# Turning gathered rows by VectorE after a trip through DRAM, in place of TensorE

## The chip, the cores and the metric

The kernel runs on one core of one Trainium2 chip. The metric is the device time of one launch in microseconds (us): the median of three runs is 1747.23 us (1746.43 to 1751.63). A further execution was recorded by the hardware profiler; all readings of the profile and of the trace are from that one execution.

The core has five instruction streams that run side by side and wait for each other by semaphores: TensorE (PE, with its weight loads shown as PEld), VectorE (DVE), ScalarE (ACT), GpSimd (POOL) and SyncE (SP). In this kernel POOL also issues the indirect DMAs (rows gathered or scattered by index), and SP issues nearly all plain DMAs. Each stream executes its instructions in the order in which they stand in the program.

## The reference

Two parts follow one another: an attention without softmax, and a mixture of eight experts on its result.

```python
scores = scale * np.matmul(z, z.transpose(0, 2, 1))          # 8 batches, 2496 tokens, 64 features
attn = np.maximum(scores, 0.0) ** 2
x = (u * np.matmul(attn, v)).reshape(N, 256)                  # N = 19968 rows

do_compute = (x @ w_skip) > 0                                 # about half of the rows
logits = xc @ w_gate                                          # xc = x[do_compute]
e_idx = np.argmax(logits, axis=1)
gate_w = softmax(logits)[e_idx]
for e in range(8):                                            # rows of one expert
    h = np.maximum(xc[mask] @ w1[e], 0.0)                     # 256 -> 1024
    y[mask] = gate_w[mask, None] * (h @ w2[e])                # 1024 -> 256
out[do_compute] = xc + y                                      # the other rows: out = x
```

## The kernel before

**Number format.** All matmuls work on fp32 values that are split into a high and a low part (tiles ending in `h` and `l`); three products (high by high, low by high, high by low) are accumulated. So whoever makes a matmul operand makes two tiles: a cast on ACT for the high part and a subtraction on DVE (or POOL) for the low part.

**Attention** (the first 1260 us or so). For each batch and each chunk of 512 queries, `scores` (L277), `weights` (L325 to L339) and `attend` (L366) run over the keys; `finish` (L379) multiplies by `u` and stores the rows to `out` and to a DRAM tensor `xr`, from which the second part reads. `kept` holds score blocks in DRAM so that the mirrored half is not computed again. `routing` (L419) finds each row's expert and writes its token number and gate weight into a DRAM list `lst`, one stretch for each expert.

**Experts** (from about 1257 us to the end). For expert `e` (0 to 7 in the code) the rows are handled in *pairs* of 2 x 128 rows. `fetch` (L576) copies the row numbers into `go` on DVE (L580) and gathers the two times 128 rows from `xr` by two indirect DMAs on POOL (L582). They arrive with one row in each partition. The first matmul needs the features in the partitions, so `turn_pe` (L592) turns each pair: four 128 x 128 transposes on TensorE into a PSUM tile `pst` (L600), a cast on ACT into the high part `xh` (L602), a subtraction on DVE into the low part `xl` (L603). The turned pair lies in `xt` or, for pair 0 of an expert, `xtf`.

**A unit** (`unit`, L605) handles up to 512 rows: parts `h_part` (L620: matmuls with `w1` into a PSUM tile `psh`, ReLU on ACT into `hh` L639, low part on DVE into `hl` L640) and `y_part` (L645: matmuls with `w2` L653), lagging by `lead` parts. There are four PSUM buffers for `psh`, so the fifth `h_part` of a unit needs the first `hl`. At the end, DVE makes `o` = gate x y + row (L682) and POOL scatters it to `out` (L685).

**Each expert** has three fixed units of 256 rows (`NFIX` = 3; pairs 0, 1, 2), called units 0, 1 and 2 here. The rest of its rows, whose number is known only at run time, is done in a branch (`tc.Switch`, L970) with one arm for each number of 64-row strips; the arm has one or two units of up to 512 rows, with pairs 3, 4 and, where needed, 5. In this data the arms of experts 1 to 7 have 8, 8, 7, 4+5, 5, 4+5 and 8+4 strips. Every engine takes the branch by itself, on entry and on leaving.

**What sets the order.** The order is written out by hand (`manual_schedule`, L786): each stream executes what the program emits, in the order of emission. `fills` names work that is slipped in between the parts of a unit: `(k, f)` emits `f` after part `k`. A fixed unit has seven parts: h0, h1, h2, h3, y, y, y are k = 0 to 6, and k = 7 stands behind them all but ahead of `o`. Before the change, unit `i` of an expert `e` from 1 on emits:

```python
add(fills, (1, rows(e, i + 3)), (3, lambda: turn_pe(pair(e, i + 1), turned(e, i + 1))))
if more:
    add(fills, (4, rows(e + 1, i)))
...
add(fills, *zip((1, 3, 5), wq[3 * i : 3 * i + 3]))
if e and more and i == 2:
    add(fills, (7, lambda: turn_pe(pair(e + 1, 0), turned(e + 1, 0))))
if i == NFIX - 1:
    add(fills, (5, lambda: turn_pe(pair(e, NFIX + 1), turned(e, NFIX), 2, 2 * P)))
```

`rows` is a `fetch`: pair `i + 3` of this expert and pair `i` of the next are gathered in unit `i`. `wq` are the eight pieces of the next expert's weights (`load_w`, L126): SP loads a piece into one of four `raw` buffers (L97), ACT casts it (L152, L158), and from expert 2's weights on POOL subtracts (L153, L159), which frees the `raw` buffer. So POOL's stream in a fixed unit holds, in this order, a gather of two, weight pieces, a second gather of two, a weight piece, and the two scatters of the unit; SP's stream holds the weight loads, each waiting for a free `raw` buffer, and one load of a list of row numbers.

## Time and profile before

| what | value |
|---|---|
| time, median of 3 runs | 1747.23 us |
| time of the profiled execution | 1763.1 us |
| its span, first to last instruction | 1761.3 us |
| granted TensorE clock | 0.996 |
| TensorE busy | 98% of the span |
| VectorE, ScalarE, GpSimd busy | 68%, 64%, 29% of the span |
| transposes of `turn_pe` on TensorE | 180 (176 into `pst`, 4 into `psm`) |
| DMA, mean over the span | 167 GB/s |

How to read it: "busy" is a share of the whole span and mixes the two parts. In the forty slices of the profile VectorE and ScalarE are at 7 to 8 tenths in the attention and at 3 to 4 in the experts, GpSimd at 1 to 3 and then 3 to 6, TensorE at 9 (that is 90% or more) in nearly all. The profiled execution took 15.9 us more than the median of the timed runs.

### The profile page before, as it was taken

The page shows a single profiled execution, that of the slowest core. Times are in us where ns is not written, and L with a number is a line of the kernel's source. Part 1 is how long each engine was busy: PE and PEld are TensorE (multiplying, and loading weights), DVE is VectorE, ACT ScalarE, POOL GpSimd, SP SyncE. Part 2 cuts the span into 40 slices and gives each one's busy share as a digit, 9 for nine tenths or more (in the row PEclk, how much of TensorE's full clock was granted, in tenths as well). Part 3 has the DMA queues.
Part 4 walks back from the last instruction along what each step waited for, and adds up shares of the span by engine and source line. Part 5 has one row for each costly group of instructions (what it writes and reads, how often), then busy time and mean ns, then how long its engine had stood idle before and what let it go on. Part 6 is the DMA issues. An engine that isn't in the chain of part 4 may idle for free.

```text
span 1761.3 us, 39302 instructions
## 1 busy us (share of the span) xinstructions
PE 1734.3 (98%) x15476; PEld 1548.9 (88%) x15476; DVE 1189.1 (68%) x1928; ACT 1130.9 (64%) x1409; POOL 517.6 (29%) x516
## 2 busy tenths in 40 slices
PE   9999999999999999999999999999899999999998
PEld 7888788988898898888899888888789999999997
DVE  6877877887787788788778877877643333433432
ACT  8877877887788788778777876877333323333321
POOL 1103212211320221232122123112345456645631
PEclk9999999999999999999999999999999999999999
DMA  5676789587778868787785888678452333323210
GB/s 193 150 181 169 193 228 255 136 232 218 206 184 215 244 157 229 224 214 177 210 258 147 225 235 215 154 209 221 133 126 76 79 96 108 87 60 98 85 40 28
DMA packets 454666, 294.71 MB, mean 167 GB/s; under 512 B 218224, under 2 KB 393201, under 8 KB 454352
## 3 DMA queue, kind: packets, MB, share of 16 engines
q1 hardware_dynamic: 440288, 267.86, 57.0%
q0 software_dynamic: 13632, 22.99, 4.7%
q8 instruction: 136, 2.23, 0.5%
q14 instruction: 178, 1.46, 0.3%
q10 hardware_dynamic: 432, 0.18, 0.0%
HBM read 157.47 MB, written 133.79 MB: 165 GB/s over the span
## 4 chain that ended last, share of the span: by engine, by line
PE 86%; DMA 5%; issue 3%; DVE 2%; ACT 2%; SPq 0%; POOL 0%; POOLq 0%; DVEq 0%; ACTq 0%
PE acc L366 53%; PE y L653 11%; PE psh L634 11%; PE ps L277 9%; DMA out<-o,idt 2%; DMA r<-kept 2%; PE psm L434 1%; DVE al L339 1%; ACT ah L335 1%; PE pst L600 1%; DMA raw<-in_v 1%; DMA kept<-rt 1%; ACT r L325 0%; ACT r L326 0%; DVE rt L294 0%
## 5 line engine op out<-in xcount | busy, mean ns | idle before, releaser
L366 PE MATMUL acc<-ah,vh 64*128 64x512 f32 (+1 forms) x3120 | 645.8, 384 | 2.6 <-DVE ah L335 2.0
L366 PE MATMUL acc<-ah,vl 64*128 64x512 f32 (+1 forms) x3120 | 630.6, 382 | 0.0
L339 DVE TENSOR_TENSOR al<-r,ah 128x1024 fp32r<-128x1024 f32 (+1 forms) x400 | 479.3, 1205 | 172.1 <-ACT ah L335 146.2
L366 PE MATMUL acc<-al,vh 64*128 64x512 f32 (+1 forms) x3120 | 500.5, 383 | 1.4 <-DVE al L339 0.5
L533 POOL DMA_INDIRECT lst<-pair,dest x160 | 198.9, 1243 | 776.8 <-DVE dest L531 745.8
L335 ACT CAST ah<-r 128x1024 fp32r<-128x1024 f32 (+1 forms) x356 | 362.6, 1029 | 82.2 <-PE acc L366 39.4
L366 PEld LDWEIGHTS acc<-ah,vh 64*128 64x128 f32 x3120 | 331.4, 184 | 51.6 <-ACT ah L335 4.5
L366 PEld LDWEIGHTS acc<-ah,vl 64*128 64x128 f32 x3120 | 331.6, 184 | 40.3 <-DVE vl L122 0.3
L366 PEld LDWEIGHTS acc<-al,vh 64*128 64x128 f32 x3120 | 314.0, 184 | 51.5 <-DVE al L339 10.1
L325 ACT ACTIVATE r<-ps 128x1024 f32<-128x1024 f32 (+1 forms) x248 | 252.5, 1018 | 143.2 <-PE ps L277 117.7
L639 ACT ACTIVATE hh<-psh 128x512 fp32r<-128x512 f32 (+2 forms) x172 | 96.3, 571 | 296.1 <-PE psh L634 247.5
L326 ACT ACTIVATE r<-r 128x1024 f32<-128x1024 f32 (+1 forms) x248 | 261.4, 1054 | 7.9
L653 PE MATMUL y<-w2t,hh 128*128 128x256 f32 (+1 forms) x1328 | 236.3, 281 | 0.0
L640 DVE SCALAR_TENSOR_TENSOR hl<-psh,hh 128x512 fp32r<-128x512 f32 (+2 forms) x172 | 110.0, 655 | 153.0 <-ACT hh L639 110.5
L294 DVE STREAM_TRANSPOSE rt<-r 128x512 f32<-128x512 f32 x304 | 197.3, 687 | 10.5 <-DMA kept<-rt 10.5
L653 PEld LDWEIGHTS y<-w2t,hh 128*128 128x128 f32 (+1 forms) x1328 | 201.9, 186 | 1.3
L634 PE MATMUL psh<-xt,w1h 128*128 128x256 f32 (+3 forms) x896 | 187.4, 306 | 10.9 <-issue 5.6
L653 PE MATMUL y<-w2t,hl 128*128 128x256 f32 (+1 forms) x664 | 184.8, 278 | 0.0
L634 PEld LDWEIGHTS psh<-xt,w1h 128*128 128x128 f32 x896 | 143.1, 190 | 18.6 <-issue 8.0
L634 PE MATMUL psh<-xt,w1l 128*128 128x256 f32 (+3 forms) x448 | 136.1, 304 | 1.4 <-issue 1.4
L685 POOL DMA_INDIRECT out<-o,idt x77 | 76.3, 991 | 171.4 <-DVE o L682 139.0
L653 PEld LDWEIGHTS y<-w2t,hl 128*128 128x128 f32 (+1 forms) x664 | 123.3, 186 | 0.0
(188 smaller groups left out, 1712.2 us busy)
## 6 DMA issues: line engine op xcount, KB each, us to landing
kept<-rt SPq DMA_DIRECT2D x304, 256.0 KB
r<-kept SPq DMA_DIRECT2D x90, 512.0 KB
r<-kept SPq DMA_DIRECT2D x62, 352.0 KB
raw<-in_v SPq DMA_DIRECT2D x80, 256.0 KB
ut<-in_uT SPq DMA_DIRECT2D x32, 512.0 KB
xr<-xrow SPq DMA_DIRECT2D x128, 128.0 KB
out<-xrow SPq DMA_DIRECT2D x128, 128.0 KB
raw<-in_w SPq DMA_DIRECT2D x64, 256.0 KB
```

The costliest lines, as they stand in the source:

```text
L277: nc.tensor.matmul(to, k[h, o : o + P], queries(ci, q, h, n), start=(m == 0), stop=(m == 2))
L294: nc.vector.transpose(t[:, :, 32 * k : 32 * k + 32].rearrange("p (k a) i -> p a k i", k=4), r[:, x, :].rearrange("p (a k i) -> p a k i", a ...
L325: nc.scalar.activation(r[:, :, :n], ps[:, :, :n], AF.Relu, scale=isc)
L326: nc.scalar.activation(r[:, :, :n], r[:, :, :n], AF.Square)
L335: (nc.scalar.copy if on_act(ci, p) else nc.vector.tensor_copy)(h_, r_)
L339: nc.vector.tensor_sub(l_, r_, f32(h_))
L366: nc.tensor.matmul(acc[t][:, :n], w[h, x, dd], a[h, x, :n], start=(first and t not in halves[:m]), stop=(last and t not in halves[m + 1 :]),)
L533: put = nc.gpsimd.indirect_dma_start(out=lst, out_offset=bass.IndirectOffsetOnAxis(ap=dest[:, t : t + 1], axis=0), in_=pair[:, t, :], in_o ...
L634: nc.tensor.matmul(ps[:, j * W : (j + 1) * W], wt[:, a, o : o + P], x[:, d, :W], start=(m == 0), stop=(m == 5),)
L639: nc.scalar.activation(hh[:, : G * W], ps[:, : G * W], AF.Relu)
L640: nc.vector.scalar_tensor_tensor(hl[:, : G * W], ps[:, : G * W], 0.0, f32(hh[:, : G * W]), op0=ALU.max, op1=ALU.subtract)
L653: nc.tensor.matmul(ys[t], h[:, tt], w2t[f][:, k, :], start=(f == 0 and m == 0 and t % share == 0), stop=(f == NF - 1 and m == 2), skip_gro ...
```

## The change

Pairs of experts 1 to 7 (the second to the eighth) are no longer turned by TensorE. Instead:

- `to_far`: SP stores the gathered pair, as it lies, into a DRAM tile `far[e % 2][i]` of 256 x 256 (one DMA of 256 KB).
- `blocks`: SP loads it back in another order, by four DMAs of 64 KB, one for each group of 64 features, into 32 partitions each (`blk`, three buffers, in the space that `ut` had): partition 32 b + i holds the features 64 b to 64 b + 63 of the rows i, i + 32, i + 64 and so on. Each DMA has 256 pieces of 256 bytes.
- `turn_dve`: DVE transposes 32 x 32 blocks of it into `raw` (128 x 512); then ACT casts and DVE subtracts, as before but from SBUF in place of PSUM.
- the rows of `w1` are permuted on the host for experts 1 to 7, so that the features' order after these blocks fits.

The gathers themselves, their places and POOL's stream stay. Expert 0 keeps `turn_pe`; so does the loop for rows beyond the longest arm, which this data does not reach.

Places: `to_far(e, i + 3)` stands at k = 5 of unit `i` (k = 4 in unit 2), `to_far(e + 1, i)` at k = 6 (k = 7 in unit 2). `blocks(e, i + 1)` stands at k = 0 of unit `i`; in unit 2 also `blocks(e, 4)` at k = 2, `blocks(e + 1, 0)` at k = 4 and `blocks(e, 5)` at k = 6. The turns stay where `turn_pe` stood. All of `to_far` and `blocks` is in SP's stream.

```diff
+    blk = []
+
+    def blocks(e, i):
+        src = far[e % 2][i].rearrange("(m i) (b f) -> b i m f", i=32, b=4)
+        x = blk[1 + (i - 1) % 2 if i else 0].rearrange("p (m f) -> p m f", f=64)
+        for b in range(4):
+            nc.sync.dma_start(x[32 * b : 32 * b + 32], src[b])
+
+    def to_far(e, i):
+        return lambda: nc.sync.dma_start(far[e % 2][i].rearrange("(t p) d -> p t d", p=P), pair(e, i))
+
+    def turn_dve(e, i, xt, o=0):
+        x = blk[1 + (i - 1) % 2 if i else 0].rearrange("p (m d j) -> p m d j", d=2, j=32)
+        raw = zp.tile([P, 2 * D], F32, name="xraw", tag="zf", bufs=3)
+        nc.vector.transpose(raw.rearrange("p (d m i) -> p m d i", d=2, i=32), x)
+        xh, xl = (x[:, :, o : o + UT] for x in xt)
+        r = raw.rearrange("p (d q) -> p d q", d=2)
+        nc.scalar.copy(xh, r)
+        nc.vector.tensor_sub(xl, r, f32(xh))
...
+    def turn(e, i, xt, o=0):
+        return (lambda: turn_dve(e, i, xt, o)) if e else (lambda: turn_pe(pair(e, i), xt, 2, o))
...
             if e:
-                add(fills, (1, rows(e, i + 3)), (3, lambda: turn_pe(pair(e, i + 1), turned(e, i + 1))))
+                add(fills, (0, to_blocks(e, i + 1)), (1, rows(e, i + 3)))
+                add(fills, (3, turn(e, i + 1, turned(e, i + 1))), (4 if i == 2 else 5, to_far(e, i + 3)))
                 if e == 1 and i == 0:
-                    add(fills, (0, rows(1, 2)))
+                    add(fills, (0, rows(1, 2)), (4, to_far(1, 2)))
                 if more:
-                    add(fills, (4, rows(e + 1, i)))
+                    add(fills, (4, rows(e + 1, i)), (7 if i == 2 else 6, to_far(e + 1, i)))
...
-            if e and more and i == 2:
-                add(fills, (7, lambda: turn_pe(pair(e + 1, 0), turned(e + 1, 0))))
+            if e and i == NFIX - 1:
+                add(fills, (2, to_blocks(e, NFIX + 1)), (6, to_blocks(e, NFIX + 2)))
+            if more and i == NFIX - 1:
+                add(fills, (4 if e else 7, to_blocks(e + 1, 0)))
+                if e:
+                    add(fills, (7, turn(e + 1, 0, turned(e + 1, 0))))
             if i == NFIX - 1:
-                add(fills, (5, lambda: turn_pe(pair(e, NFIX + 1), turned(e, NFIX), 2, 2 * P)))
+                add(fills, (5, turn(e, NFIX + 1, turned(e, NFIX), 2 * P)))
...
+    w1 = np.concatenate([moe_w1[:1], moe_w1[1:, cols]])
```

In the last fixed unit of expert 0, `to_far(1, 0)` and `to_far(1, 1)` stand at k = 5 and 7 and `blocks(1, 0)` at k = 7; pair 0 of expert 1 is turned in the first unit of expert 0's arm, at k = 1. In the two-unit arms the pairs of the second unit are turned by `turn_dve` at k = 3 and 5 of the first.

More of the change, by code (lines that the diff above doesn't have):

```diff
@@ L85, in attn_moe @@
     lst = dram.tile([E * CAP, 2], I32, name="lst")
+    far = [[dram.tile([UT, D], F32, name="far%d%d" % (k, i)) for i in range(NSTAT)] for k in range(2)]
     zt, vt = {}, {}
@@ L866, in attn_moe @@
     row_tiles("u", 4)
+    blk += [xp.tile([P, 2, QC], F32, name="blk", tag="ut", bufs=3)[:, 0, :] for _ in range(3)]
     xtf += [zp.tile([P, 2, 2 * P], F32R, name="xtf", tag="zl", bufs=ZBUFS) for _ in range(2)]
@@ L979, in attn_moe @@
             if e == 0 and not ws:
-                turn_pe(pair(1, 0), turned(1, 0))
+                turn(1, 0, turned(1, 0))()
             for j, hw in enumerate(ws):
@@ L985, in attn_moe @@
                 if e == 0 and j == 0:
-                    add(fills, (1, lambda: turn_pe(pair(1, 0), turned(1, 0))))
+                    add(fills, (1, turn(1, 0, turned(1, 0))))
                 while there < min(i + 3, end - 1):
                     there += 1
-                    add(fills, (1, rows(e, there)))
+                    add(fills, (1, rows(e, there)), *([(3, to_far(e, there))] if e else []))
                 if after:
                     xt = xts[(NFIX + j + 1) % 2]
-                    add(fills, (3, lambda nxt=nxt, xt=xt: turn_pe(pair(e, nxt), xt)))
-                    if after[0] > 4:
-                        add(fills, (5, lambda nxt=nxt, xt=xt: turn_pe(pair(e, nxt + 1), xt, 2, 2 * P)))
+                    for k in range(2 if after[0] > 4 else 1):
+                        if e and nxt + k > NFIX + 2:
+                            add(fills, (4 * k, to_blocks(e, nxt + k)))
+                        add(fills, (3 + 2 * k, turn(e, nxt + k, xt, 2 * P * k)))
                 w = -(-hw // 2)
```

23 lines of the change are left out of this document (16 added, 7 removed).

## The prediction

> **What bounds the kernel now.** I read the page's busy line first, then its slices, then the timeline of TensorE in one expert.
>
> ```profile
> PE 1734.3 (98%) x15476; PEld 1548.9 (88%) x15476; DVE 1189.1 (68%) x1928; ACT 1130.9 (64%) x1409; POOL 517.6 (29%) x516
> ...
> PE   9999999999999999999999999999899999999998
> ...
> POOL 1103212211320221232122123112345456645631
> ```
>
> TensorE is busy nearly without a gap, so what is taken from it is won, unless it has to wait for something new. POOL's 29% is an average over two parts; in the experts it is the next fullest. How full it is in the fixed units shows only in the expert itself. I take the fourth expert (e = 3), whose unit 0 begins at 1448.46. Columns of the first row: stretch, length, then busy us of each engine:
>
> ```profile
> 1456.00:1490.00 34.00, 33.23 (x271) 32.54 (x270) 13.07 (x26) 12.34 (x27) 28.93 (x30) 1.00 0.48 132
> ...
> 1448.46 0.40 PE L634 MATMUL psh<-xtf,w1h 128*128 128x256 f32 x2
> ...
> 1456.48 1.05 POOL L582 DMA_INDIRECT xgu<-xr,go  x1 [3.19 <-DVE go L580]
> ...
> 1479.86 1.04 POOL L582 DMA_INDIRECT xgu<-xr,go  x1 [0.31 <-issue]
> 1481.20 1.02 POOL L582 DMA_INDIRECT xgu<-xr,go  x1 [0.30 <-issue]
> ```
>
> POOL has 28.93 us of work in 34, and 0.3 us of issue before each gather or scatter (the last rows), so from 1456.48 on it has nothing to spare. It starts its first gather 8.0 us after TensorE has begun unit 0 (1448.46) and stays that late: the gather of pair 5, emitted after part 1 of unit 2, starts its second half only at 1481.20. Today nobody minds, because pair 5 is turned in the arm or not at all.
>
> Next, the end of unit 2 and the start of the arm on TensorE and VectorE:
>
> ```profile
> 1483.68 0.60 PE L600 MATMUL pst<-ident,xgf 128*128 128x128 f32 x4
> 1484.03 0.65 PE L634 MATMUL psh<-xt,w1h 128*128 128x448 f32 x2
> ...
> 1488.77 0.36 PE L634 MATMUL psh<-xt,w1l 128*128 128x448 f32 x1
> 1489.90 0.67 PE L634 MATMUL psh<-xt,w1h 128*128 128x448 f32 x2 [0.77 <-DVE hl L640]
> ```
>
> ```profile
> 1484.94 0.69 DVE L603 TENSOR_TENSOR xtf<-pst,xtf 128x512 fp32r<-128x512 f32 x1 [1.42 <-ACT xtf L602]
> 1485.54 0.87 DVE L682 SCALAR_TENSOR_TENSOR o<-y,idt,xgf 128x256 f32<-128x256 f32 x2
> 1489.22 2.22 DVE L640 SCALAR_TENSOR_TENSOR hl<-psh,hh 128x448 fp32r<-128x448 f32 x4 [2.81 <-ACT hh L639]
> ```
>
> TensorE goes from unit 2 into the arm without a pause, does the four `h_part`s for which there is PSUM, and then waits for the first `hl`. That comes 4.28 us after VectorE began the low part of `xtf` (1484.94 to 1489.22): the two `o`, and the branch, in which VectorE stands still for 2.81 us though ScalarE was the one named. So the turn of the next expert's pair 0, last before the branch, already decides when TensorE goes on, and TensorE has under a microsecond of slack there (0.77 us lost).
>
> **The change part by part.** *Removed:* the transposes. What a turn costs TensorE is read between neighbours:
>
> ```profile
> 1454.22 0.60 PE L600 MATMUL pst<-ident,xgf 128*128 128x128 f32 x4
> 1454.57 0.48 PE L653 MATMUL y<-w2t,hh 128*128 128x256 f32 x2
> ...
> L600 PE MATMUL pst<-ident,xgf x92: 270/272/328, 1259.3 to 1703.0; 128*128 128x128 f32 x92
> ...
> L600 PE MATMUL pst<-ident,xgu x84: 270/272/273, 1298.0 to 1726.6; 128*128 128x128 f32 x84
> ```
>
> Four transposes take 1454.57 - 1454.22 = 0.35 us of TensorE's stream. 92 + 84 = 176 are 44 turns; four of them (pairs 1 to 4 of expert 0) stay, so 40 go: 40 x 0.355 = 14.2 us, if nothing is put in their place.
>
> *Added on VectorE and ScalarE:* a block transpose a turn, for which the attention has the same shape; the cast and the subtraction stay.
>
> ```profile
> L294 DVE STREAM_TRANSPOSE rt<-r x304: 660/686/714, 46.4 to 1219.1; 128x512 f32<-128x512 f32 x152
> ...
> L602 ACT CAST xt<-pst x37: 582/583/587, 1263.1 to 1727.0; 128x512 fp32r<-128x512 f32 x37
> ```
>
> 0.69 us, five to seven times an expert, on an engine that was busy 13.07 of 34 us: nothing, beside the wait. The cover is the y parts of the same unit.
>
> *Added on SP:* five DMAs a turn, in a stream that so far held only weight loads. These rows price them:
>
> ```profile
> 1389.62 0.97 POOL L685 DMA_INDIRECT out<-o,idt  x1 [0.95 <-issue]
> 1392.29 0.97 POOL L685 DMA_INDIRECT out<-o,idt  x1 [1.70 <-DMA out<-o,idt]
> ...
> 1423.72 3.49 DMA xgu<-xr,go
> ...
> 1248.02 2.21 SPq L412 DMA_DIRECT2D xr<-xrow  x4
> ...
> 1192.73 5.95 DMA r<-kept
> ```
>
> A 128 KB indirect transfer is through 1392.29 - 1389.62 = 2.67 us after its start, or 1.70 us after its issue has ended; a gather that meets the next weights' loads takes 3.49 us (chain of waits). For gathers I take 2.67, as those weight loads now stand behind it in SP's stream. SP issues four stores of 256-byte pieces, of 128 KB each, in 2.21 us, 0.55 each; a load of 64 KB has half the pieces, so four cost between 1.1 and 2.2 us; I take 1.6. The trace has no load of 256-byte pieces. Its landing after the last issue is at least the 1.70 above and at most 5.95 - 0.55 = 5.4 (512 KB in the full queues of the attention); the experts' queues are half empty (DMA share 0.48), so I take 2.2, near the low end.
>
> *The wait.* SP works in order. In unit 2 it has, one behind the other, `blocks(e, 3)`, `blocks(e, 4)`, `to_far(e, 5)`, `blocks(e + 1, 0)`. The third must wait for the gather of pair 5, though the fourth needs nothing of it: its rows were put away two units earlier. And VectorE meets the fourth in the last turn ahead of `o` and the branch. So, with F the start of the second half of that gather:
>
> F + 0.5 (POOL a little later, below) + 2.67 (gather lands) + 0.55 (`to_far` issued) + 1.6 + 2.2 (`blocks(e + 1, 0)`) = F + 7.5: data there. Then 0.69 (block transpose) + 0.59 (cast) + 4.28 (low part, `o`, branch) = F + 13.1: first `hl` of the arm. For e = 3: 1481.20 + 13.1 = 1494.3 instead of 1489.22, 5.1 us late. The other experts, by their own rows:
>
> ```profile
> 1366.32 1.01 POOL L582 DMA_INDIRECT xgu<-xr,go  x1 [0.30 <-issue]
> ...
> 1425.07 1.01 POOL L582 DMA_INDIRECT xgu<-xr,go  x1 [0.30 <-issue]
> ...
> 1539.50 1.01 POOL L582 DMA_INDIRECT xgu<-xr,go  x1 [0.30 <-issue]
> ...
> 1602.33 1.01 POOL L582 DMA_INDIRECT xgu<-xr,go  x1 [0.30 <-issue]
> ...
> 1656.35 1.01 POOL L582 DMA_INDIRECT xgu<-xr,go  x1 [0.30 <-issue]
> ```
>
> ```profile
> 1372.13 2.48 DVE L640 SCALAR_TENSOR_TENSOR hl<-psh,hh 128x512 fp32r<-128x512 f32 x4 [3.43 <-ACT hh L639]
> ...
> 1431.12 1.29 DVE L640 SCALAR_TENSOR_TENSOR hl<-psh,hh 128x512 fp32r<-128x512 f32 x2 [2.98 <-issue]
> ...
> 1546.43 1.89 DVE L640 SCALAR_TENSOR_TENSOR hl<-psh,hh 128x512 fp32r<-128x512 f32 x3 [2.55 <-issue]
> ...
> 1609.97 1.69 DVE L640 SCALAR_TENSOR_TENSOR hl<-psh,hh 128x320 fp32r<-128x320 f32 x4 [2.96 <-issue]
> ...
> 1662.31 1.89 DVE L640 SCALAR_TENSOR_TENSOR hl<-psh,hh 128x512 fp32r<-128x512 f32 x3 [1.96 <-ACT hh L639]
> ```
>
> F + 13.1 against these: e = 1, 7.3; e = 2, 7.1; e = 4, 6.2; e = 5, 5.5; e = 6, 7.1 us. In e = 4 and 6 the arm begins with a 256-row unit, and what needs the first `hl` (0.69 us long) is its first `y`:
>
> ```profile
> 1547.59 0.48 PE L653 MATMUL y<-w2t,hh 128*128 128x256 f32 x2
> ...
> 1664.03 0.36 PE L653 MATMUL y<-w2t,hh 128*128 128x256 f32 x1
> ```
>
> That leaves 0.5 and 1.0 us of slack, which I take off: 5.7 and 6.1. Sum over six experts: 7.3 + 7.1 + 5.1 + 5.7 + 5.5 + 6.1 = 36.8 us. This is a loss of TensorE's time one for one, since the next expert's start, POOL's exit from the arm and so the next F all hang on the end of the arm: the loop now runs arm, POOL, SP, VectorE, branch, arm.
>
> Two waits of the same kind lie inside it and cost nothing more.
>
> ```profile
> 1462.90 1.00 POOL L582 DMA_INDIRECT xgf<-xr,go  x1 [0.30 <-issue]
> ...
> 1467.21 0.68 DVE L603 TENSOR_TENSOR xt<-pst,xt 128x512 fp32r<-128x512 f32 x1
> ```
>
> `blocks(e, 2)` stands behind `to_far(e + 1, 0)`, whose gather starts its second half at 1462.90 and lands at 1465.6; SP is through at 1466.1, the data there at 1469.9, while VectorE, which made the low part at 1467.21, asks a little before that. Behind the waiting VectorE and ScalarE stand the row numbers of the next gather and weight casts, for which POOL waits: the 0.5 us above (0 to 2, by the two ends of the prices). `blocks(e, 3)` and `(e, 4)` are late for unit 2 and the arm by two or three us, but the arm waits longer for `hl`. The next weights' loads, which now stand behind all this on SP, have the whole arm to land.
>
> Turns that really come off TensorE's time are thus only those outside the waiting stretches: pair 0 of expert 1, two each in the arms of e = 4 and 6, five of e = 7 (no next expert, POOL's stream short, SP on time): 10 x 0.355 = 3.6 us. Net: + 36.8 - 3.6 = + 33.2 us on the profiled execution's 1763.1, that is 1796.3. The timed median is 15.9 us below that execution, so I put the difference on it: 1747.2 + 33 = **1780 us**.
>
> The Trainium skill, page "DMA: Bandwidth & Descriptors", section "Anatomy of one DMA", gives 2.0 us plus bytes / 436 GB/s for a transfer. By it a gather half would take 2.3 in place of 2.67 us and `blocks` would be there 0.4 us sooner, an estimate of 0.8 us an expert and about 1775 us. The row 2.67 is measured here and the loads have small pieces, so the sum stays with the rows.
>
> Bounds for one expert: lowest 0 + 2.67 + 0.28 (half an issue) + 1.1 + 1.7 = 5.75 in place of 7.5, six times 1.75 less: 1770. Highest 2 + 3.49 + 0.55 + 2.2 + 5.4 = 13.6: 37 us more, 1817.
>
> **Rivals.** *A: the waits are covered, the change does what it removes.* All that would be needed is that `blocks(e + 1, 0)` is there before TensorE ends unit 2 (1483.7 in e = 3). Then 14.2 us go, and up to about 1 us an expert more, since VectorE reaches the branch without waiting for `pst`: 1747 - 14 to 20, say 1732 (faster). It decides from F + 7.5 falling about 5 us earlier. For it: the profiled execution is 15.9 us longer than the timed ones, and if that sits in POOL's stream and the branches, F lies earlier when nothing is recorded. Against it: the gather of pair 5 alone lands after 1483.7 by its rows, and `to_far` must follow it.
>
> *B: half covered.* If the unrecorded POOL gains about 3 us an expert, each wait shrinks to 2 or 3 us: 6 x 2.5 - 3.6 = + 11, about 1758; with 5 us gained it ends within noise of before.
>
> *C: small pieces are dear.* If the loads of 256-byte pieces take the 5.4 us or more, the wait grows to 10 us and more an expert and the VectorE waits in units 0 and 1 reach TensorE too: from 1800 up to 1817 or more. For it: 1024 pieces a turn; against it: the half-empty queues.
>
> **How the numbers follow.** My forecast (SP blocked behind the gather of pair 5; 1762 to 1800) 0.64; C 0.13; B 0.12, of which 0.05 within 0.3% of before (5 us, about what a measurement of this kernel can tell from no change); A 0.11. Faster 0.11, same 0.05, slower 0.84. The range 1755 to 1808 holds the forecast, most of B and half of C, about 0.8.
>
> **What would show it.** Right: in the waits of the experts, VectorE waits before the block transposes for a DMA into `blk`, longest for the one ahead of each branch; TensorE's `psh` waits for `hl` grow from 1 to some 6 us in six experts; SP's own longest waits are for the gathered `xgu`; between two experts' first `xtf` matmuls the distance grows by 5 to 7 us. Wrong: these distances shrink by 1.8 us or more (A); VectorE asks after the data are there; SP reaches `blocks(e + 1, 0)` before the gather has landed; or `blocks` itself takes over 5 us from issue to use (C).

## The result and the profile after

The changed kernel takes 1827.07 us (median of 4 runs, 1825.43 to 1829.36); beside it, on the same chip, the kernel before took 1749.24 us (1746.43 to 1751.63). The ratio is 1.0454, 95 % interval 1.0437 to 1.0471: 78 us slower. The forecast was 1780 us with a range of 1755 to 1808: the right direction, and less than half of the size.

The line numbers of the second part have moved: `fetch` is L581 and L583, `blocks` L614, `to_far` L617, the block transpose L623, the cast and the low part behind it L626 and L627, the matmuls of `h_part` L658 and of `y_part` L677, `hh` L663, `hl` L664, `o` L706.

From the page of the changed kernel: busy time, the granted clock in 40 slices, and the shares of the chain that ended last by engine.

```profile
PE 1742.6 (96%) x15316; PEld 1544.2 (85%) x15316; DVE 1219.8 (67%) x1968; ACT 1134.5 (62%) x1409; POOL 516.4 (28%) x516
...
PEclk9999999999999999999999999999989899899999
...
PE 73%; DMA 13%; issue 4%; DVE 3%; ACT 3%; SPq 2%; POOL 1%; POOLq 0%; DVEq 0%; ACTq 0%
```

TensorE has 160 instructions fewer (15316 for 15476, the 40 turns) and yet 8 us more busy time, and its clock has dents among the experts. DMA now holds 13 % of the chain, where the kernel before had 5 %. Who waits, in the experts from 1300 us on (total us, times, longest), first on the engines, then on SP's queue:

```profile
DVE xraw L623 <- DMA blk<-far: 88.7, 26, 11.4
...
PE psh L658 <- ACT xt L626: 33.6, 6, 8.6
...
PE psh L658 <- DVE hl L664: 6.5, 4, 2.6
```

```profile
SPq L617 <- DMA xgu<-xr,go: 193.0, 21, 28.9
SPq L617 <- DMA xgf<-xr,go: 97.4, 19, 20.7
```

SP stands 290 us at the writes to DRAM, each waiting for its rows to be gathered; VectorE stands 89 us before block transposes; and what stops TensorE most is not `hl`, as the forecast had it, but the cast of a turned pair. (The view puts another 17.0 us before `psh` down to "issue"; the stop ahead of the arm, below, is one of these.)

The fourth expert (e = 3) once more, on TensorE. Its unit 0 starts in the first row, the next expert's in the last; 70.81 us, where the kernel before took 57.37 (1448.46 to 1505.83).

```profile
1464.07 0.40 PE L658 MATMUL psh<-xtf,w1h 128*128 128x256 f32 x2
...
1486.48 0.28 PE L677 MATMUL y<-w2t,hl 128*128 128x256 f32 x1
1492.27 1.31 PE L658 MATMUL psh<-xt,w1h 128*128 128x256 f32 x2 [5.51 <-ACT xt L626]
...
1509.53 1.42 PE L658 MATMUL psh<-xt,w1h 128*128 128x448 f32 x2 [2.87 <-issue]
...
1518.94 0.68 PE L658 MATMUL psh<-xt,w1h 128*128 128x448 f32 x2 [1.41 <-DVE hl L664]
...
1520.26 0.39 PE L677 MATMUL y<-w2t,hh 128*128 128x256 f32 x2
...
1534.88 0.40 PE L658 MATMUL psh<-xtf,w1h 128*128 128x256 f32 x2
```

There are three stops: 5.5 us ahead of unit 2, 2.9 us ahead of the arm, 1.4 us for the first `hl`. The same stretches as windows (stretch, length, busy us of PE, PEld, DVE, ACT, POOL, then granted clock, DMA share and GB/s):

```profile
1486.40:1492.30 5.90, 0.39 (x5) 0.18 (x3) 0.76 (x2) 0.70 (x2) 2.02 (x2) 0.94 0.83 224
1492.30:1501.00 8.70, 8.56 (x48) 8.26 (x49) 3.95 (x8) 3.53 (x9) 7.14 (x9) 0.65 0.35 107
1501.00:1506.60 5.60, 5.60 (x50) 5.47 (x49) 2.94 (x5) 1.83 (x4) 4.83 (x6) 1.00 0.84 149
1506.60:1509.50 2.90, 0.07 (x1) 0.00 (x0) 0.75 (x2) 0.62 (x1) 2.27 (x3) 0.85 0.56 142
1509.50:1520.30 10.80, 9.36 (x31) 7.82 (x32) 4.89 (x9) 2.47 (x5) 2.03 (x2) 0.72 0.54 150
```

The 48 h matmuls of unit 2 take 8.7 us at a mean clock of 0.65; over their first 5.4 us it is 0.50:

```profile
1492.30:1497.70 5.40, 5.26 (x23) 4.96 (x24) 2.72 (x5) 1.74 (x5) 4.62 (x6) 0.50 0.31 87
```

The kernel before did its stretch from the arm's first h to its first y in 7.2 us, with the clock at 1.00:

```profile
1484.10:1491.30 7.20, 6.43 (x33) 5.65 (x32) 3.56 (x7) 2.55 (x5) 5.00 (x6) 1.00 0.49 159
```

So the 13.4 us that this expert lost are: 5.5 idle ahead of unit 2, 3.2 in unit 2's h (8.7 instead of the 5.5 that the same matmuls take in unit 1, 1475.48 to 1480.95), 2.9 idle ahead of the arm, 3.6 in the arm's first h (10.8 instead of 7.2), less five turns of 0.355 = 1.8. That makes 13.4. Why each stop is there, from VectorE, POOL and SP (start, duration, issue or operation; idle time before it in brackets):

```profile
1490.85 0.71 DVE L623 STREAM_TRANSPOSE xraw<-blk 128x512 f32<-128x512 f32 x1 [8.33 <-DMA blk<-far]
...
1508.07 0.71 DVE L623 STREAM_TRANSPOSE xraw<-blk 128x512 f32<-128x512 f32 x1 [1.88 <-DMA blk<-far]
...
1513.19 0.71 DVE L623 STREAM_TRANSPOSE xraw<-blk 128x512 f32<-128x512 f32 x1 [3.04 <-DMA blk<-far]
...
1518.26 2.21 DVE L664 SCALAR_TENSOR_TENSOR hl<-psh,hh 128x448 fp32r<-128x448 f32 x4 [2.19 <-ACT hh L663]
```

```profile
1482.87 0.37 SPq L617 DMA_DIRECT2D far<-xgf  x1
1483.29 1.49 SPq L575 DMA_DIRECT2D idt<-lst  x1
1484.83 3.08 SPq L614 DMA_DIRECT2D blk<-far  x4
...
1498.88 0.38 SPq L617 DMA_DIRECT2D far<-xgf  x1
1499.96 4.20 SPq L614 DMA_DIRECT2D blk<-far  x8
1507.33 0.39 SPq L617 DMA_DIRECT2D far<-xgu  x1
1507.82 4.36 SPq L614 DMA_DIRECT2D blk<-far  x8
```

```profile
1502.30 1.01 POOL L583 DMA_INDIRECT xgu<-xr,go  x1 [0.30 <-issue]
```

Every read (`blk<-far`) comes out of SP right behind a write that has waited. `blocks(e, 2)` (1484.83) stands behind `to_far(e + 1, 0)` (1482.87); `blocks(e, 3)` and `(e, 4)` (1499.96) behind `to_far(e + 1, 1)` (1498.88); `blocks(e + 1, 0)` (1507.82) behind `to_far(e, 5)` (1507.33). The first makes unit 2 late, the second the arm, the third the first `hl`.

### The profile page after: what moved, and what is told of

It is laid out like the page before. It is cut to its first block, busy times and chain, and to the rows that moved or that the text cites. A ratio compares the mean times of both kernels' runs of the same rounds, so it can differ in the third digit from the quotient of the medians.

```text
span 1823.6 us, 39434 instructions
## 1 busy us (share of the span) xinstructions
PE 1742.6 (96%) x15316; PEld 1544.2 (85%) x15316; DVE 1219.8 (67%) x1968; ACT 1134.5 (62%) x1409; POOL 516.4 (28%) x516
## 4 chain that ended last, share of the span: by engine, by line
PE 73%; DMA 13%; issue 4%; DVE 3%; ACT 3%; SPq 2%; POOL 1%; POOLq 0%; DVEq 0%; ACTq 0%
PE acc L367 54%; PE ps L278 9%; DMA xgf<-xr,go 7%; PE psh L658 4%; PE y L677 4%; DMA blk<-far 2%; DMA out<-o,idt 2%; SPq L614 1%; PE psm L435 1%; DVE al L340 1%; ACT ah L336 1%; DVE xraw L623 1%; DMA kept<-rt 1%; DMA xgu<-xr,go 1%; DMA raw<-in_w 0%
## 5 line engine op out<-in xcount | busy, mean ns | idle before, releaser
L367 PEld LDWEIGHTS acc<-ah,vl 64*128 64x128 f32 x3120 | 330.5, 184 | 42.7 <-DVE vl L123 0.3
L658 PE MATMUL psh<-xt,w1h 128*128 128x256 f32 (+3 forms) x896 | 204.8, 324 | 59.9 <-ACT xt L626 33.6
L663 ACT ACTIVATE hh<-psh 128x512 fp32r<-128x512 f32 (+2 forms) x172 | 95.9, 571 | 245.1 <-PE psh L658 241.2
L677 PE MATMUL y<-w2t,hh 128*128 128x256 f32 (+1 forms) x1328 | 236.8, 281 | 6.9 <-ACT hh L663 6.9
L658 PEld LDWEIGHTS psh<-xt,w1h 128*128 128x128 f32 x896 | 156.5, 207 | 72.2 <-ACT xt L626 34.8
L664 DVE SCALAR_TENSOR_TENSOR hl<-psh,hh 128x512 fp32r<-128x512 f32 (+2 forms) x172 | 110.2, 655 | 152.9 <-ACT hh L663 140.5
L677 PEld LDWEIGHTS y<-w2t,hh 128*128 128x128 f32 (+1 forms) x1328 | 204.1, 187 | 8.6 <-ACT hh L663 7.3
L677 PE MATMUL y<-w2t,hl 128*128 128x256 f32 (+1 forms) x664 | 186.4, 281 | 1.2 <-DVE hl L664 1.2
L658 PE MATMUL psh<-xt,w1l 128*128 128x256 f32 (+3 forms) x448 | 142.5, 318 | 0.0
L677 PEld LDWEIGHTS y<-w2t,hl 128*128 128x128 f32 (+1 forms) x664 | 123.5, 186 | 1.7 <-DVE hl L664 1.7
```

What stands on the lines that cost most here:

```text
L367: nc.tensor.matmul(acc[t][:, :n], w[h, x, dd], a[h, x, :n], start=(first and t not in halves[:m]), stop=(last and t not in halves[m + 1 :]),)
L658: nc.tensor.matmul(ps[:, j * W : (j + 1) * W], wt[:, a, o : o + P], x[:, d, :W], start=(m == 0), stop=(m == 5),)
L663: nc.scalar.activation(hh[:, : G * W], ps[:, : G * W], AF.Relu)
L664: nc.vector.scalar_tensor_tensor(hl[:, : G * W], ps[:, : G * W], 0.0, f32(hh[:, : G * W]), op0=ALU.max, op1=ALU.subtract)
L677: nc.tensor.matmul(ys[t], h[:, tt], w2t[f][:, k, :], start=(f == 0 and m == 0 and t % share == 0), stop=(f == NF - 1 and m == 2), skip_gro ...
```

## The experiments

Three theories were set against each other. BRANCH is the one on record: the next expert's pair 0, behind the write of pair 5, makes the first `hl` of the arm late, and that is the loss. ORDER: the same mechanism, but at the other reads, above all pair 2 between units 1 and 2, with the half clock and a late POOL in its train. PRICE: pieces of 256 bytes make the reads themselves slow. Later CLOCK: the half clock after each stop is a large part. The runs fell on several chips, on which the kernel before took 1746 to 1762 us; so each is given as a ratio to the kernel before on its own chip (0.01 is 17.5 us; the changed kernel stands at 1.0454).

**1. Pair 2's read earlier.**

```diff
-                add(fills, (0, to_blocks(e, i + 1)), (1, rows(e, i + 3)))
+                if i != 1 or e == 1:
+                    add(fills, (0, to_blocks(e, i + 1)))
+                if i == 0 and e > 1:
+                    add(fills, (0, to_blocks(e, 2)))
+                add(fills, (1, rows(e, i + 3)))
```

> Changed kernel with one move: in experts 2 to 7 of the code's count, blocks(e, 2) is issued in unit 0 right behind blocks(e, 1), so it no longer stands behind to_far(e + 1, 0) and its gather. Theory ORDER (the loss sits first where VectorE waits for pair 2: TensorE idle 5.9 us between units 1 and 2, then 6.8 us at half clock, and GpSimd some 5 us late): the idle time and the slow clock behind it go in five experts, the waits for pairs 3 and 4 remain; 1827 less about 7 us in five experts, near 1790. Theory BRANCH (the one on record: the first hl behind the branch decides): 1820 to 1827. Theory PRICE (loads of 256-byte pieces are slow in themselves): 1815 to 1827.

Measured: 1804.18 us, ratio 1.0330 (1.0313 to 1.0348). In e = 3 the stop ahead of unit 2 is gone (it begins 22.5 us into the expert, 23.2 before the change), but the arm begins at 41.4 instead of 35.6 us. Neither forecast met it: the stop at pair 2 is real, and something else takes over most of what it gave back.

**2. The next pair 0 ahead of pair 5's write.**

```diff
-                add(fills, (4 if e else 7, to_blocks(e + 1, 0)))
+                add(fills, (2 if e else 7, to_blocks(e + 1, 0)))
```

> Changed kernel with one move: blocks(e + 1, 0) stands at k = 2 of unit 2, ahead of to_far(e, 5) and its gather, and no longer behind it. Theory BRANCH: the wait that decides is gone, 5 us or more in six experts, near 1795. Theory ORDER: TensorE's idle stretches at units 1 to 2 and 2 to arm stay as they are and only part of the arm's start is won, 0 to 2 us an expert, 1815 to 1827. Theory PRICE: 1820 to 1827.

Measured: 1817.09 us, ratio 1.0398 (1.0373 to 1.0423). The wait on which the forecast had put everything is out of the way, and an eighth of the loss comes back. BRANCH alone is not the cause of 78 us.

**3. The reads ahead of the writes that they do not need** (the same DMAs, for e from 2 on; the next pair 0's read still stands behind the write of pair 4).

```diff
+                    add(fills, *((0, to_blocks(e, k)) for k in ((1, 2), (3,), ())[i]))
...
+                    add(fills, (4, rows(e + 1, i)))
+                    add(fills, *((k, to_far(e + 1, j)) for j, k in ((), ((0, 1),), ((1, 4), (2, 7)))[i]))
...
+                add(fills, (0, to_blocks(e, NFIX + 1)), (6, to_blocks(e, NFIX + 2)))
...
+                add(fills, (0 if e else 7, to_blocks(e + 1, 0)))
```

> Changed kernel with SP's stream in another order and nothing else: each blocks stands ahead of the to_far that it does not need (pairs 1 and 2 in unit 0, pair 3 at the start of unit 1, pair 4 and the next expert's pair 0 at the start of unit 2; to_far of the next expert's pairs 0, 1, 2 at the start of unit 1, k = 4 and k = 7 of unit 2); the same DMAs, bytes and pieces. Theories ORDER and BRANCH: no wait is left beyond expert 1, TensorE keeps the 14 us of its transposes: 1730 to 1740, faster than before. Theory PRICE: the pieces are as slow as they were, above 1790.

Measured: 1766.39 us, ratio 1.0117 (1.0095 to 1.0138), above the 1730 to 1740 expected. With the same bytes in the same pieces three quarters of the loss are gone, so it is the order. What was left, from its waits after 1390 us:

```profile
ACT w2t L159 <- DMA raw<-in_w: 25.1, 7, 5.1
...
DVE xraw L623 <- DMA blk<-far: 16.5, 9, 4.6
```

The next expert's weight pieces now stood behind the writes on SP and came late to ScalarE: the same mechanism again, with another victim.

**4. Reads of long pieces**, 2 KB a partition.

```diff
-        src = far[e % 2][i].rearrange("(m i) (b f) -> b i m f", i=32, b=4)
-        x = blk[1 + (i - 1) % 2 if i else 0].rearrange("p (m f) -> p m f", f=64)
+        src = far[e % 2][i].rearrange("(b i m) d -> b i (m d)", b=4, i=32)
+        x = blk[1 + (i - 1) % 2 if i else 0]
```

> Changed kernel with the four loads of blocks reading 2 KB pieces (contiguous rows of far) in place of 256-byte ones; same number of DMAs, same bytes, same places. The rows come in another order, so the experts' values are other ones and the work is the same. Theory PRICE: the waits for blocks shrink by half or more, 1770 to 1795. Theories ORDER and BRANCH: the gathers' waits in SP's stream stay; a transfer is some tenths of a us quicker, 1815 to 1827.

Measured: 1821.81 us, ratio 1.0435 (1.0418 to 1.0453), against 1.0454: some 3 of the 78 us come back. As other waits could hide a quicker read, look at the reads themselves. In e = 3 of this run pair 2 has:

```profile
1479.19 4.65 SPq L614 DMA_DIRECT2D blk<-far  x4
...
1485.62 0.71 DVE L623 STREAM_TRANSPOSE xraw<-blk 128x512 f32<-128x512 f32 x1 [7.01 <-DMA blk<-far]
```

From the first issue to the block transpose that is 6.4 us, where the short pieces took 6.0 (1484.83 to 1490.85); for the next pair 0 it is 5.3 us against 5.4. So the reads are dearer than the 3.8 us of the forecast (1.6 + 2.2), but not for their pieces: PRICE falls.

**5. POOL's needs ahead of the turn.**

```diff
+                add(fills, *zip((1, 3), wq[3 * i : 3 * i + 2]))
+                if more:
+                    add(fills, (3, rows(e + 1, i)))
+                add(fills, *zip((3,), wq[3 * i + 2 : 3 * i + 3]))
                 add(fills, (3, turn(e, i + 1, turned(e, i + 1))), (4 if i == 2 else 5, to_far(e, i + 3)))
...
-                add(fills, *zip((1, 3, 5), wq[3 * i : 3 * i + 3]))
```

> Only the order inside a step: the weight pieces' casts on ScalarE and the next expert's gather come ahead of the turn instead of behind it, so that ScalarE and GpSimd go on while VectorE waits for its blocks. ORDER: the wait for pair 2 between units 1 and 2 stays (about 6 us a expert), but GpSimd is not late, the second half of pair 5's gather comes some 5 us earlier and with it pair 4's blocks: 3 to 7 us an expert, 1785 to 1805. BRANCH as recorded took GpSimd as late by 0.5 us only and so expects 1820 to 1827; PRICE the same.

Measured: ratio 1.0479 (1.0450 to 1.0507), no gain, where 1785 to 1805 us were expected. In e = 3 the arm begins 2.1 us sooner than in the changed kernel (43.4 for 45.5 us), but its first y comes at 55.9 for 56.2: the gather of pair 5 did not move (38.2 us in both, 9 to 10 us behind the start of unit 2, as before the change), so the next pair 0 did not either. POOL's lateness is a consequence of unit 2's, not a cause of its own.

**6. TensorE kept busy in the stops.**

```diff
+    def warm_pe(xg, n):
+        ps = ps_acc.tile([P, 2, 2 * P], F32, name="warm", tag="acc")
+        for m in range(n):
+            t, d = divmod(m % 4, 2)
+            nc.tensor.transpose(ps[:, d, t * P : (t + 1) * P], xg[:, t, d * P : (d + 1) * P], ident)
...
+            if e and more and i:
+                add(fills, (7, lambda: warm_pe(pair(e, i), 56 if i == 1 else 32)))
```

> Work is added and nothing taken away: 56 transposes of no use (some 5 us of TensorE) behind unit 1 and 32 (some 3 us) behind unit 2 of experts 2 to 7, where TensorE stood idle waiting for a turn. CLOCK (half of the loss is TensorE at half clock for 3.4 to 6.8 us after each idle stretch): the rows at 0.5 go, and the time falls by up to 3 us a stretch, to 1795 to 1815, though work is added. If the half clock is only a mark of the idle time and costs nothing: 1827 to 1850.

Measured: ratio 1.0457 (1.0428 to 1.0486), the same as without. Windows of e = 3 (columns as above): the filled stop, unit 2's h, its y, and (behind the second filled stop) the arm up to its first y.

```profile
1495.80:1501.80 6.00, 6.00 (x58) 6.00 (x57) 1.27 (x2) 1.21 (x4) 1.51 (x3) 1.00 0.75 216
1501.80:1507.40 5.60, 5.60 (x51) 5.60 (x50) 3.52 (x8) 3.04 (x8) 4.95 (x7) 1.00 0.26 76
1507.40:1513.10 5.70, 5.70 (x51) 5.70 (x50) 1.00 (x2) 0.60 (x1) 4.76 (x6) 1.00 0.52 148
...
1518.80:1529.80 11.00, 7.55 (x31) 6.32 (x32) 4.98 (x9) 2.47 (x5) 3.30 (x4) 0.91 0.53 150
```

The h of unit 2 is back at 5.6 us and full clock, 3.1 us better, and unit 2 ends 2.6 us sooner. But the arm begins 45.5 us into the expert, to the tenth as in the changed kernel, for pairs 3 and 4 are not there earlier (VectorE waits 5.52 us ahead of pair 3's block transpose). The mean clock of the whole execution went from 0.979 to 0.987, so part of the half clock is left; what was taken away gained nothing, for the next late read swallowed it. That speaks against CLOCK as a cause.

**7. Without the trip.**

```diff
     def blocks(e, i):
+        if e > 1 or i > 2:
+            return
...
     def to_far(e, i):
+        if e > 1 or i > 2:
+            return lambda: None
```

> Left out: the writes to DRAM and the reads back for experts 3 to 8, and for pairs 3 to 5 of expert 2; VectorE turns what its buffer last held, so the output's values are others, while TensorE, VectorE and ScalarE have the same instructions as in the changed kernel. This is the ceiling of the change: TensorE without its 40 turns and no trip to wait for. All theories: far below 1827; the arithmetic of the prediction (14.2 us of TensorE removed, of which 3.6 to 14.2 come off) gives 1732 to 1744. If it stays above 1760, VectorE's transposes themselves or the place of the turn cost, and neither ORDER nor PRICE is the whole.

Measured: ratio 0.9950 (0.9936 to 0.9965), 9 us faster than the kernel before. This is what TensorE's 40 turns are worth when nothing is waited for: more than the 3.6 us that the forecast let come off, less than 14.2.

**8. All legs spread out.** Weight pieces first; each gather, write, read and turn about half a unit behind the one before it.

```diff
+                if i == 0:
+                    add(fills, (0, to_blocks(e, 1)))
...
+                    add(fills, (1, rows(e, 3)), (4 if e == 1 else 1, to_far(e, 2)), (6, rows(e, 4)))
+                    add(fills, (6, to_blocks(e, 2)), (7, to_far(e, 3)))
+                    if more:
+                        add(fills, (4, rows(e + 1, 0)))
+                elif i == 1:
+                    if more:
+                        add(fills, (1, to_far(e + 1, 0)), (4, rows(e + 1, 1)))
+                    add(fills, (3, to_far(e, 4)), (4, to_blocks(e, 3)), (5, rows(e, 5)), (7, to_blocks(e, 4)))
+                    if more:
+                        add(fills, (7, to_blocks(e + 1, 0)))
+                else:
+                    if more:
+                        add(fills, (2, rows(e + 1, 2)), (1, to_far(e + 1, 1)))
+                    add(fills, (4, to_far(e, 5)))
```

> The same transfers and turns as in the changed kernel, each issued in another place: every leg of a pair's trip (gather, write, read back, turn) gets about half a unit (some 6 us) or more of its own, nothing on SP stands behind a wait that it does not need, and the weight pieces stand ahead of the pair's trip. ORDER: the whole loss goes, and with it the stretches at half clock: 1735 to 1750 us, periods of experts as before the change or 1 to 2 us below, since the 40 turns no longer cost TensorE anything there. The order with all reads first still lost 20 us, mostly to weight loads behind SP's waits and to pairs 3 and 4, so this one has to fall below its 1766. PRICE (the bytes and the pieces themselves slow everything): over 1780 whatever the order.

Measured: ratio 1.0006 (0.9989 to 1.0023). The whole loss is gone, with every transfer of the changed kernel still made; as gathers have moved on POOL too, this run is not of SP's order alone. From the waits of its experts:

```profile
DVE xraw L623 <- DMA blk<-far: 14.5, 10, 3.3
```

89 us of waiting for reads have become 14.5. SP still stands 111 us at the writes (66.5 + 44.7, against 290): such a wait costs little where no read that is soon needed stands behind it.

**9. The same, with pair 4's gather sooner** (against run 8).

```diff
-                    add(fills, (1, rows(e, 3)), (4 if e == 1 else 1, to_far(e, 2)), (6, rows(e, 4)))
+                    add(fills, (1, rows(e, 3)), (4 if e == 1 else 1, to_far(e, 2)), (2, rows(e, 4)))
...
-                        add(fills, (4, rows(e + 1, 0)))
+                        add(fills, (6, rows(e + 1, 0)))
...
-                        add(fills, (1, to_far(e + 1, 0)), (4, rows(e + 1, 1)))
-                    add(fills, (3, to_far(e, 4)), (4, to_blocks(e, 3)), (5, rows(e, 5)), (7, to_blocks(e, 4)))
+                        add(fills, (4, rows(e + 1, 1)))
+                    add(fills, (0, to_far(e, 4)), (0, to_blocks(e, 3)), (5, rows(e, 5)), (5, to_blocks(e, 4)))
+                    if more:
+                        add(fills, (2, to_far(e + 1, 0)))
```

> The spread order once more, with pair 4's gather ahead of the next expert's first gather, so that its whole trip starts some 5 us sooner. In the spread order the experts 2, 3 and 7 still had arms that began 1 to 2.6 us late or whose first h came late, 3.4, 2.5 and 3.3 us a period above the kernel before, and the experts in between ran 1 to 2.5 us below it. ORDER: these three come down by 1 to 3 us each: 0.3 to 0.5 % below the kernel before (ratio 0.995 to 0.998), the ceiling being the run without the trip, 0.995. If the rest is the traffic itself: ratio 0.999 to 1.002, as the spread order.

Measured: 1757.79 us beside 1762.10, ratio 0.9982 (0.9970 to 0.9993). This order is 0.2 % below the kernel before, hardly more than a measurement can tell; the reads are waited for 6.6 us in all, but ScalarE again waits for weight pieces:

```profile
ACT w2t L159 <- DMA raw<-in_w: 35.6, 12, 7.3
...
DVE xraw L623 <- DMA blk<-far: 6.6, 2, 4.8
```

**10. Moves 1 and 2 together** (both diffs above).

> The two single moves of before together: pair 2's read in unit 0, and the next expert's first read ahead of the write that waits for pair 5's gather. Apart they gave 23 and 10 us of 78 back. If the waits stand in a row, each with its own cover, and hide one another (ORDER in the wide sense: pair 2, pair 4 and the next pair 0), the two together give more than the sum, 40 to 60 of 78 (ratio 1.010 to 1.022); if they are independent costs, 33 (ratio 1.026); if either decides alone, no more than 23 (1.032).

Measured: ratio 1.0298 (1.0273 to 1.0324), 52 us: hardly below move 1 alone. So a third wait decides by then. In e = 3 unit 2 begins at 22.5 us, in time, and the arm at 42.7, late by 7.1:

```profile
1503.36 7.20 SPq L614 DMA_DIRECT2D blk<-far  x12
...
1509.66 0.71 DVE L623 STREAM_TRANSPOSE xraw<-blk 128x512 f32<-128x512 f32 x1 [8.71 <-DMA blk<-far]
```

This is pair 3, whose read neither move touched: it stands behind the write of the next expert's pair 1 (1502.07). Pair 4 and the next pair 0 are turned right behind it, without a wait.

**11. The reads on ScalarE's queue, at the same places.**

```diff
-            nc.sync.dma_start(x[32 * b : 32 * b + 32], src[b])
+            nc.scalar.dma_start(x[32 * b : 32 * b + 32], src[b])
```

> One word is changed: the block reads are issued on ScalarE's queue in place of SP's, at the same places of the program; the writes stay on SP. So a read no longer stands behind a write that waits for another pair's gather, and waits for nothing but its own pair's write and its buffer. ORDER (it is the shared queue, not the place or the bytes): pairs 1, 2 and the next pair 0 are there in time, pairs 3 and 4 late by 0 to 3 us, and ScalarE pays 4 issues of about 0.45 us a pair, partly between its casts: 1750 to 1780 (ratio 1.00 to 1.02). If the place in the program is what is late: ratio 1.035 to 1.05. PRICE: 1.04.

Measured: ratio 1.0288 (1.0257 to 1.0318), above the 1.02 expected. From its waits:

```profile
ACT hh L663 <- DMA blk<-far: 40.7, 14, 6.6
ACT hh L663 <- DMA far<-xgf: 19.7, 4, 6.3
```

Unit 2 of e = 3 begins in time (23.3 us for 23.2 before the change), so the reads no longer stand behind the writes; but the reads now hold up ScalarE's ReLUs behind them, by their issue (1.8 us and more for four) and where they wait for their own pair's write. The wait has moved to another stream that works in order.

**12. Only the next expert's writes later.** They go behind the reads of pairs 2 and 4; pair 5's write stays ahead of the next pair 0, as in the forecast.

```diff
-                    add(fills, (4, rows(e + 1, i)), (7 if i == 2 else 6, to_far(e + 1, i)))
+                    add(fills, (4, rows(e + 1, i)))
+                    if i:
+                        add(fills, (2 * i, to_far(e + 1, i - 1)))
+                    if i == 2:
+                        add(fills, (7, to_far(e + 1, i)))
```

> Only the two writes to DRAM of the next expert's pairs 0 and 1 are issued later: behind the reads of pair 2 and of pair 4, which they do not feed and which stood behind them. The write of pair 5 still stands ahead of the next pair 0's read, as the recorded forecast took it. So this leaves the one wait that the forecast counted, and takes away the two that it put at nothing. If the forecast's working of that one wait was right (36.8 us late, less the turns that come off), the ratio is 1.015 to 1.025 (33 us of 1747 is 1.019), units 2 begin some 22.5 us into an expert, as before the change, and the arms' first y matmuls come 4 to 7 us late. If that one is much dearer, the ratio stays at 1.03 or above; if the lateness of pairs 3 and 4 has another cause than these writes, likewise, and the arms' first h matmuls still come 5 us or more late.

Measured: 1819.54 us, ratio 1.0405 (1.0386 to 1.0424). Units 2 begin 22.5 to 26.1 us into the experts, so that stop is all but gone, and the arms' first h come 0 to 8 us late; yet the loss is still 71 us, where some 33 were expected. Its e = 3, on SP, VectorE and TensorE:

```profile
1498.99 0.39 SPq L617 DMA_DIRECT2D far<-xgu  x1
1499.49 0.40 SPq L617 DMA_DIRECT2D far<-xgf  x1
1500.02 4.47 SPq L614 DMA_DIRECT2D blk<-far  x8
```

```profile
1505.34 0.71 DVE L623 STREAM_TRANSPOSE xraw<-blk 128x512 f32<-128x512 f32 x1 [5.73 <-DMA blk<-far]
...
1510.34 2.22 DVE L664 SCALAR_TENSOR_TENSOR hl<-psh,hh 128x448 fp32r<-128x448 f32 x4 [2.12 <-ACT hh L663]
```

```profile
1494.13 1.01 POOL L583 DMA_INDIRECT xgu<-xr,go  x1 [0.30 <-issue]
```

```profile
1460.74 0.40 PE L658 MATMUL psh<-xtf,w1h 128*128 128x256 f32 x2
...
1511.01 1.11 PE L658 MATMUL psh<-xt,w1h 128*128 128x448 f32 x2 [6.44 <-DVE hl L664]
```

Here the forecast's picture stands nearly by itself (the arm's first h is 2.6 us late), with TensorE 6.44 us at the arm's first `hl`. Its F is 1494.13, 33.4 us into the expert; the forecast had 32.74 + 0.5 = 33.2. From F on it is longer than worked out: the gather 4.86 us to the write's issue (forecast 2.67), the write, the moved write (0.5, which this edit adds) and the reads 6.35 up to the block transpose (0.55 + 1.6 + 2.2 = 4.35), then 5.00 to the first `hl` (5.56). That is 16.2 us from the gather's start to the first `hl`, where the forecast had 12.6 (its F + 13.1 less the half us for POOL).

**13. With the next pair 0 ahead of pair 5's write as well.**

```diff
-                add(fills, (4 if e else 7, to_blocks(e + 1, 0)))
+                add(fills, (3 if e else 7, to_blocks(e + 1, 0)))
```

> The same with the next pair 0's read one step ahead of the write of pair 5: all three waits gone with three moves, everything else as in the changed kernel. If the three are the whole of the loss: ratio 0.997 to 1.008, and the move that alone gave 10 us of 78 gives here the 20 us or more that the wait costs when nothing else hides it. If something of the loss is left that is not among the three: 1.01 or above.

Measured: 1784.71 us, ratio 1.0199 (1.0181 to 1.0218). The move that gave 10 us by itself (there one step earlier, at k = 2) gives 36 here. But 0.997 to 1.008 was expected, so it was not the last: in e = 3 VectorE still stops for pair 3, whose read stands behind the write of pair 4.

```profile
1487.11 0.72 DVE L623 STREAM_TRANSPOSE xraw<-blk 128x512 f32<-128x512 f32 x1 [2.76 <-DMA blk<-far]
```

```profile
1479.41 0.37 SPq L617 DMA_DIRECT2D far<-xgu  x1
...
1481.93 6.44 SPq L614 DMA_DIRECT2D blk<-far  x12
```

How the places compare in one expert (e = 3; us from its first `xtf` matmul to the start of unit 2, the first h and the first y of the arm, and the next expert, each read from TensorE's timeline), beside the ratio of the whole kernel:

| kernel | unit 2 | arm's h | arm's y | next expert | ratio |
|---|---|---|---|---|---|
| before | 23.2 | 35.6 | 42.8 | 57.4 | 1 |
| changed | 28.2 | 45.5 | 56.2 | 70.8 | 1.0454 |
| pair 2 early (1) | 22.5 | 41.4 | 49.5 | 64.1 | 1.0330 |
| next pair 0 early (2) | 27.1 | 44.1 | 52.3 | 67.0 | 1.0398 |
| both (10) | 22.5 | 42.7 | 51.4 | 66.1 | 1.0298 |
| POOL first (5) | 29.2 | 43.4 | 55.9 | 71.5 | 1.0479 |
| TensorE kept busy (6) | 28.6 | 45.5 | 56.5 | 71.8 | 1.0457 |
| ScalarE's queue (11) | 23.3 | 40.3 | 50.7 | 66.0 | 1.0288 |
| writes late (12) | 23.3 | 38.2 | 52.7 | 68.1 | 1.0405 |
| writes late, next pair 0 early (13) | 23.1 | 39.1 | 48.1 | 62.7 | 1.0199 |
| reads first (3) | 22.5 | 34.5 | 42.7 | 57.6 | 1.0117 |
| spread (8) | 22.5 | 33.6 | 41.5 | 56.2 | 1.0006 |
| no trip (7) | 22.5 | 33.6 | 40.9 | 55.6 | 0.9950 |

## Why the prediction was right or wrong

**Right: the direction and the kind of cause.** A write that waits at the head of SP's stream for a gather that it alone needs holds up reads that need nothing of it. Runs 3 and 8 show it: the same transfers cost 20 us, then 1 us, when the reads are taken out from behind such waits.

**Failed: "Two waits of the same kind lie inside it and cost nothing more."** This step failed in two ways. For pair 2 the forecast had the data there at 1469.9, 21.4 us into the expert; with block transpose and cast (0.69 + 0.59) that makes 22.7, half a us before unit 2 began (23.2). They came 26.8 us into the expert, 8.3 us after VectorE asked, and VectorE is the only way to unit 2's operand, so TensorE stood 5.5 us. The 0.5 us for "POOL a little later" should have been 5.5: in the changed kernel F is 1502.30 - 1464.07 = 38.2 us into the expert, against 32.74. Pairs 3 and 4 were to hide behind the wait for `hl`; in run 10, where the two others are out of the way, pair 3 makes the arm 7.1 us late. The 5.3 us by which pair 2 came later than worked out can be read in SP's rows: the write waits to 1482.87, 1.7 us later in the expert than worked out; the load of row numbers that stands between, and was in no term, takes 1.5 us; the four reads take 3.1 us to issue for 1.6, and land 2.9 us after that for 2.2. TensorE was through at 1486.5.

Neither this step nor the size of the counted wait makes the 78 us alone. Without the counted wait some 70 remain (run 2). Without the next expert's writes ahead of pairs 2 and 4 some 71 remain (run 12), where the forecast's sum would leave 33. The stops cover one another, so either group nearly suffices; run 12's arms still begin up to 8 us late, so it is not quite the counted wait alone.

**Mis-sized: F + 13.1.** Run 12 has F in its place and measures 16.2 us behind it in e = 3 instead of 12.6. Of the 3.6 us more, 2.2 are the gather, for which the choice was 2.67 between 2.67 and 3.49. It took 4.86 there and 5.03 in the changed kernel (1502.30 to 1507.33). The row that gave 2.67 was not of a gather at all but of a scatter (`out<-o,idt`) in a stretch with a DMA share of 0.19 (1389.50 to 1392.30). By the packets in the trace of the kernel before, pair 5's gather in e = 3 already ran for 3.9 us there (last packet at 1485.06; 3.9 to 4.7 us in the six experts), and for 4.4 in the changed kernel, so the price was low from the start and not for the new traffic. What makes such a gather slow stays open: the DMA share was 0.51 in run 12's stretch and 0.83 in the changed kernel's. The upper bound of the sum held this price too low as well. The other terms of the 3.6 are 1.5 for write and reads and 0.5 for the write that run 12 moved there, less 0.6 behind the block transpose. In the changed kernel the first `hl` comes 1518.26 - 1464.07 = 54.2 us into the expert, 13.4 later than before (40.8) where 5.1 was forecast. The 8.3 more are 5.0 from F, 2.4 from the gather, 1.5 from write and reads (5.86 for 4.35), less 0.5 behind the block transpose.

**How the 78 us divide.** Not as a sum: the waits stand one behind the other, and each covers part of the next. Taken away one after the other they leave 1.0454 as changed; 1.0405 without the next expert's writes ahead of pairs 2 and 4; 1.0199 without pair 5's write ahead of the next pair 0; 1.0006 with pairs 3 and 4 and the weight pieces freed too, in an order that moves gathers as well; 0.9950 with no trip at all. The wait that the forecast counted is the step from 1.0405 to 1.0199, 36 us, close to the 36.8 worked out, but by luck: its terms were too small, and a cover that was not seen made up for it. Taken away first, the wait gives 10 (run 2). Of the step from 1.0199 to 1.0006 the shares of pair 3, pair 4 and the weights were not measured apart.

**The half clock** was in nobody's sum. In e = 3 TensorE goes on slowly after both long stops: a mean of 0.65 over 8.7 us behind 5.9 us of idleness, 0.72 over 10.8 us behind 2.9. Run 6 shows that it can be avoided ahead of unit 2, and that this gains nothing here. The Trainium skill, page "TensorE: Matmul & The Clock Gate", section "What's actually happening" of its part 1, says that an idle window of about 3.4 us puts the clock at half and that sustained work of about as long brings it back; the trace agrees for the long stop (5.9 us, then 0.50 over 5.4 us); the short one, 2.9 us and so less than that window, was enough too, with a mean clock of 0.85 already within it.

**The cost of the block transpose** was right: 0.71 us each (0.69 forecast), and in run 7, where only it is left, nothing is lost. **The turns that come off**: of the 3.6 us only the last expert's share can be read (2.1 us for 1.8); where the waits are gone all forty count for about 9 us (run 7).

**The figure of the Trainium skill.** By the Trainium skill, page "DMA: Bandwidth & Descriptors", section "Anatomy of one DMA", the forecast put a gather half at an estimated 2.3 us; these traces differ, with 4.86 and 5.03 us. The other 0.4 us that the forecast took off by it, for `blocks`, does not follow: a load of 64 KB comes to 2.15 us by that figure, against the 2.2 of the sum.

**The announced signs.** VectorE does wait before block transposes for DMAs into `blk`, and SP longest for `xgu`, as said. `blocks` takes over 5 us from issue to use (6.0 and 5.4 us in e = 3), which was to be the sign of C; run 4 shows that it comes without small pieces too. The wait ahead of the branch is not the longest, that for pair 2 is (8.33 against 3.04 us in e = 3). TensorE's wait for `hl` did not grow to 6 us in the changed kernel (1.4 us in e = 3), because unit 2 and the arm were late already; in run 12, with these in place, it is 6.44. The distances between experts grew by 9.5 to 16 us instead of 5 to 7 (e = 1 to 6); the last expert, which has no next one, became 2.1 us shorter up to its last y (67.2 for 69.3), as forecast.

**The rivals.** A (all covered) and B (half covered) are refuted by the time; C (small pieces dear) by run 4, though its "1800 up to 1817 or more" holds the measured time, and though VectorE's waits did reach TensorE as it said. What spoke for A and B, the 15.9 us by which the profiled execution exceeded the median, seems not to lie in POOL's stream and the branches: the expert e = 1 begins at 1329.36 there, and at 1317.06 in the changed kernel's profile, so most of it lies ahead of the experts that the change touches. The other side of the forecast, A, is what orders 8 and 9 come near to: it needed not a quicker POOL but another order on SP.

## What to carry to other kernels

Before a transfer is added to a stream that works in order, write that stream down with what each entry waits for, and ask of every entry behind a wait when it is needed; a wait of the same kind counts nothing only if its data are there before TensorE runs out, with a margin wider than the doubt in the prices (here it was half a us). When several such waits follow one another, removing one shows little: the first to go gave 10 or 22 of 78 us here, and the move that gave 10 gave 36 once others had gone, so they have to be taken out in combination before a cause is dismissed. A trip through DRAM with three legs cost here no more than the turns that it replaced (1.0006 and 0.9982, against 0.9950 with no trip), once each leg had its own stretch of the schedule and nothing that others soon need stood behind it.
